# A new explicit order for the first task list of a fused attention and state-space kernel

## The chip, the cores and the metric

The kernel runs on one core of a Trainium2 chip. Time is device microseconds of one execution. The core's engines are TensorE (PE, with its weight loads PEld), VectorE (DVE), ScalarE (ACT), GpSimd (POOL) and SyncE (SP). Each engine takes its instructions strictly in the order in which the program lists them, and waits at an instruction until what that instruction depends on is there; everything behind it on that engine waits too. DMAs are issued from three queues here: SP's, POOL's and a few from ACT's.

## The reference

The input `x` has 2048 rows of 640. Two branches read it, and a gate mixes them:

```python
g = sigmoid((x * gate_w).sum(-1, keepdims=True))
a = attention(x)       # 32 heads of 20; each position sees 8 keys, 0, 2, .. 14 rows back
b = state_space(x)     # convolution with K[d, l] = Re sum_n C dt B exp(dt A l), plus x * Dskip
out = g * a + (1 - g) * b
```

Attention is `qkv = x @ wqkv`, a softmax over the eight logits of each position and head, the weighted sum of values, and `@ wo`. The state-space branch builds K for 640 channels and 2048 lags from 192 complex modes per channel, and convolves by an FFT of length 4096. All is in bfloat16 with float32 sums.

## The kernel before, in words

The work is cut into small tasks. A task has a name, an engine (or a choice of ACT and DVE), the tasks it depends on, the ring slots that it takes and releases, and a function that writes its instructions. There are two lists. The first has 1090 tasks, ends with the first FFT stage, and is what the change touches; the second has 237 (the rest of the convolution, the mix and the stores) and is the same before and after.

The order of the first list is written out by hand: `SEQ1` is a string of task numbers. `Plan.order` walks it, and a letter A or D behind a number says on which of ACT and DVE that task runs. `Plan.emit` calls the tasks in that order and ties each engine's instructions to the one before, so that no later stage reorders them:

```python
for k in self.pr["seq"]:
    t = self.tasks[int(k.rstrip("AD"))]
    t.eng = k[-1] if k[-1] in t.dur else next(iter(t.dur))
```

So the string decides three things: the order on each of PE, ACT, DVE, POOL and SP; which evictions run on ACT and which on DVE; and, with them, which waits are exposed.

The tasks that the text speaks of, with their numbers:

- 0 to 73 are the parameters of the state-space branch, on ACT and DVE. `mk` rounds a piece on ACT, `sp` (SP, line 614) writes it to `Sprm` in DRAM; sp9 is task 73, the last. `lin` (line 597 on DVE, 599 on ACT) are linear steps of this part, free to run on either.
- L00 and L01 (516, 517; SP, line 721) load the two halves of the first argument matrix L from `Sprm`; L10 and L11 (562, 563) the second, and so on to L91. `arg` (PE, line 748) multiplies by L, `act` (ACT, lines 760 and 762) takes sine or exponential, `pq` (DVE, lines 783 to 785) multiplies both, three instructions in one task, `kmm` (PE, line 801) contracts. There are ten chunks; pq92 (982) is the last product, fin9 (984) collects the last chunk.
- `late` (PE, line 291) are the 60 projections to q, k and v, `lev` their evictions. lst02, lst12, lst22 and lst32 (POOL, line 317; lst12 is 156) store v to `vS` in DRAM. gst (227) stores the gate row `omS`. halo1 to halo3 (POOL, line 312; halo2 is 177) copy keys over a block edge.
- wld (221; POOL, line 263) loads `wo` with two DMAs.
- `vc` (POOL, line 345) loads a block of shifted values from `vS` with two DMAs: vc0 (228), vc256 (264, the "second vc"), on to vc1280 (408), vc1536 (444) and vc1792 (480). Two buffers.
- The attention core has eight blocks of 256 rows. `prod` (DVE, line 351; five per block; prod74 is 489, the last) multiplies q and k, `lg` (PE, line 357) sums the heads, ast0 (244) stores the probabilities and asb0 (245) reads them back spread over partitions (SP, lines 396 and 401), `pv` (DVE, line 420; pv00, pv02, pv04 for block 0, pv50 is 426, pv60 is 462) weighs the values and needs both `asb` and `vc`, `oT` evicts (512 or 256 columns), `wo` projects (wo700 is 507), `ga` scales and evicts 320 columns on ACT (line 453) or DVE (line 455).
- The kernel K is expanded in two halves: shift, move, near, own, other (other0 is 750, other1 is 989), then `xst` stores X to `Kx` in DRAM and `xld` loads `kc` back (xst0 751 and 752, xld0 753 and 754, xst1 990 and 991, xld1 992 and 993; one of each pair on SP, one on POOL, lines 875, 873 and 881).
- rows0 to rows7 (995 to 1002; POOL, line 946) load `Usb`, the rows of x for the FFT. rows0 waits for prod74, since `Usb` takes the memory that q and k had; each later one first copies two elements of the block before (`pace`, line 945), so that it goes out only after that block has landed.
- `f1`, `fu` and `fk` (PE, line 1232) are the first FFT stage of the first half of K, of x and of the second half of K, ten, twenty and ten of them; `f1e`, `fue` and `fke` evict 1024 columns on ACT or DVE (lines 470 and 472).

When the last of these has released its PSUM, the second list starts with the `fp` matmuls (line 1009).

Of the kernel before, what the change touches and what calls it, by code (L numbers as in the profile page):

```python
# [62 lines left out]
0 2 3 1 6 8 4 14 13 26 5 7 27 9 10D 11D 12 18 74 76 28 75A 77A 78 79A 82 80 83D 15 17 23 81A 114 115D 120 94 56 121D 19 20 21 88 116 95A 89A 117A 37 100 92 104 101A 29  # L63
105A 93A 22 24 34D 35D 31 36 39 42 108 109A 25 86 118 106 90 119A 102 107A 32 103A 87A 110 96 84 16 38 30 111A 135 45 97A 40 33 46 41 136A 98 99A 43 44 229 51D 52 47 53
60 62D 122 146 85A 123A 57 147A 91A 125 129 230 126A 61 63 112 48 130A 113A 50 231 59 64A 152 154 153A 65A 155A 67 139 222 232 66 233 49 58 69 54 140A 68 70 55 71 72 234
127 137 73 235 128A 236 143 237 138A 223 144A 516 238 133 265 239 131 134D 240 148 267 224 132A 241 242 150 225 149A 151A 226 243 266 269 517 244 563 562 245 518 520 268
141 270 519 521 271 522 524 272 523 273 994 124 221 145 228 264 156 525 274 526 528 167 275 301 168D 142A 527 529 276 530 532 531 533 178 534 536 180 535 537 179A 303 538
540 539 541 175 181D 246 176D 186 542 544 277 278 543 545 187A 279 182 546 548 302 304 157 554 305 307 547 183A 549 158A 159 184 160A 306 308 550 552 551 553 185D 309 337
173 280 609 281 608 227 177 188 310 564 566 171 311 174A 565 312 567 313 172A 161 314 568 570 162A 569 571 556 315 339 165 572 574 338 573 575 166D 341 555 340 576 577
578 342 169 343 345 579 170A 163 580 582 199 581 583 584 586 585 587 557 344 346 558 588 590 589 591 200A 249 164D 559 347 600 373 203 592 594 593 204A 595 348 210 211A  # L70
205 560 596 598 206D 375 561 349 597 207 208D 350 201 351 189 602 599 202A 190A 610 612 611 613 601 374 376 377 614 616 247 615 617 379 618 620 191 248A 619 621 622 624
378 380 197 623 192A 625 626 628 252 381 605 409 198A 627 629 603 604 630 631 632 606 633 634 635 382 636 216 212 411 383 607 637 213D 646 316 655 352 654 317 638 217A
639 640 384 250 642 641 385 251A 643 644 645 214 386 656 648 387 195 215A 657 658 660 647 253 410 412 196A 659 661 254A 701 700 388 662 664 663 665 193 194A 282 651 413
666 667 668 255 257 670 256D 218 669 671 672 673 649 674 675 285 258D 415 219D 676 677 650 678 679 414 680 681 682 259 683 684 686 685 687 652 688 689 692 417 416 209 300
690 418 702 691 703 704 261 705 260A 706 708 283 707 709 710 653 694 445 419 262A 288 711 712 693 714 713 715 284D 447 697 716 718 717 719 695 720 721 722 420 724 723 725
755 756 263 353 726 727 286 289 728 729 730 696 732 731 733 734 698 421 735 318 287D 290D 738 699 736 291 737 757 758 759 760 739 761 762 422 763 765 764 766 740 423 743
# [1235 lines left out]
```

## Time and profile before

| | |
|---|---|
| median of three runs | 361.38 us (357.0 to 361.77) |
| the profiled execution | 360.97 us, of which the span is 359.0 us |
| DVE busy | 311.5 us, 87% of the span |
| ACT busy | 303.0 us, 84% |
| PE busy | 293.7 us, 82% |
| POOL busy | 78.3 us, 22% |
| first list, from the span's start to the first `fp` matmul | 283.3 us |

Times within the profile are counted from the span's start. A row of the timeline has the start, the duration, the engine, the line, the operation and its operands (out<-in), and in brackets how long the engine stood idle before and what ended that. SPq, POOLq and ACTq are the sequencers that issue DMAs: such a row is the issuing alone, and the transfer lands later. A row of the groups has the busy time and the mean of one instruction in nanoseconds, then the idle time before them.

### The profile page before, as it was taken

What the parts mean: (1) busy time and instruction counts of PE and PEld (TensorE: products, weight loads), DVE (VectorE), ACT (ScalarE), POOL (GpSimd) and SP (SyncE); (2) the same over time, 40 slices, a digit from 0 to 9 for tenths busy, and PEclk for the clock granted to TensorE, in tenths of its full rate; (3) what the DMA queues carried; (4) which work ended last, traced back from release to release, by engine and by line L of the source; (5) the groups of instructions that cost most, each with busy time, mean ns of one, the idle gap of its engine ahead of it and who ended that gap; (6) DMA issues with size and microseconds to landing.
All of it is one profiled execution on the core that took longest, in us unless ns stands there. A gap on an engine that the chain in (4) does not pass through costs nothing. (4 is left out here: it accounts for less than half of the span.)

```text
span 359.0 us, 12203 instructions
## 1 busy us (share of the span) xinstructions
PE 293.7 (82%) x5271; PEld 173.4 (48%) x5286; DVE 311.5 (87%) x413; ACT 303.0 (84%) x417; POOL 78.3 (22%) x125
## 2 busy tenths in 40 slices
PE   0199999699999999888887869999997799978760
PEld 0065564234544545445443424566664556647650
DVE  2899999669999899999998987999993479999982
ACT  1699997578989999999997979999895599888881
POOL 8930090211020100100012122416010023310032
PEclk9999999989999999999998978999998899999995
DMA  7951289421501611461256867489653149943047
GB/s 259 370 175 57 82 213 268 120 66 19 150 11 27 122 40 19 140 129 30 71 109 192 190 152 137 95 177 256 172 153 101 38 126 225 228 95 75 4 98 199
DMA packets 44042, 46.60 MB, mean 130 GB/s; under 512 B 24517, under 2 KB 38133, under 8 KB 43733
## 3 DMA queue, kind: packets, MB, share of 16 engines
q1 hardware_dynamic: 36116, 24.43, 26.2%
q0 software_dynamic: 5840, 20.55, 22.5%
q10 hardware_dynamic: 2032, 0.85, 0.9%
q8 instruction: 41, 0.67, 0.8%
q14 instruction: 13, 0.10, 0.1%
HBM read 31.31 MB, written 14.51 MB: 128 GB/s over the span
## 5 line engine op out<-in xcount | busy, mean ns | idle before, releaser
L291 PE MATMUL tb<-bufA 128*128 128x512 bf16 x285 | 71.7, 387 | 2.8 <-issue 1.1
L748 PE MATMUL ar<-Rarg,L 64*128 64x304 bf16 (+1 forms) x480 | 55.3, 282 | 14.7 <-ACT big L760 5.9
L760 ACT ACTIVATE big<-ar 128x608 bf16<-128x608 int16 x96 | 59.0, 681 | 8.2 <-PE ar L748 5.7
L762 ACT ACTIVATE big<-ar 128x864 bf16<-128x864 f32 x60 | 50.3, 917 | 3.6 <-PE ar L748 3.3
L291 PEld LDWEIGHTS <-bufA 128*128 128x128 bf16 x300 | 33.2, 120 | 31.7 <-issue 9.3
L420 DVE TENSOR_TENSOR pv<-vc,asb 128x4096 bf16<-128x4096 bf16 (+1 forms) x24 | 46.3, 1928 | 1.4 <-PE tb L426 1.4
L748 PEld LDWEIGHTS <-L 64*128 64x128 bf16 x480 | 21.4, 94 | 48.8 <-issue 41.9
L1009 PEld LDWEIGHTS <-PHI 128*128 128x128 bf16 x288 | 26.8, 99 | 18.0 <-issue 8.4
L801 PE MATMUL kps<-qq,pt 128*32 128x22 bf16 (+1 forms) x2560 | 26.3, 175 | 4.2 <-issue 4.2
L444 PE MATMUL tb<-wo_sb,oT 128*128 128x320 bf16 x160 | 28.1, 311 | 0.0
L801 PEld LDWEIGHTS <-pt 128*32 128x32 bf16 (+1 forms) x2560 | 22.5, 91 | 11.6 <-issue 8.7
L351 DVE TENSOR_TENSOR prod<-qk 128x2048 bf16<-128x2048 bf16 x20 | 24.1, 1220 | 2.9 <-PE lg L357 2.8
L351 DVE TENSOR_TENSOR prod<-prj 128x2048 bf16<-128x2048 bf16 x20 | 24.0, 1219 | 0.6 <-PE lg L357 0.5
L345 POOL DMA_DIRECT2D vc<-vS x16 | 11.5, 725 | 57.1 <-DVE pv L420 54.0
L426 PE MATMUL tb<-pv,ind 128*64 128x512 bf16 (+1 forms) x192 | 22.4, 361 | 0.2
L785 DVE TENSOR_TENSOR qq<-big 128x1408 bf16<-128x1408 bf16 x24 | 21.2, 885 | 0.0
L470 ACT ACTIVATE bufA<-bp 128x1024 bf16<-128x1024 f32 x16 | 16.0, 1032 | 5.6 <-PE bp L1232 5.5
L1009 PE MATMUL fp<-big,PHI 128*128 128x320 bf16 x112 | 17.9, 304 | 3.0 <-ACT sp_u L470 3.0
L200 PE MATMUL ar<-ident,xn 128*128 128x128 bf16 x80 | 8.1, 263 | 15.0 <-DMA xn<-in_A_x_dram 14.3
L470 ACT ACTIVATE sp_u<-fp 128x1280 bf16<-128x1280 f32 x14 | 17.3, 1237 | 3.4 <-PE fp L1009 3.4
L470 ACT ACTIVATE prj<-tb 128x512 bf16<-128x512 f32 x28 | 17.1, 612 | 3.1 <-PE tb L291 3.0
L470 ACT ACTIVATE big<-bp 128x1024 bf16<-128x1024 f32 x19 | 18.6, 1023 | 1.0 <-PE bp L1232 0.8
(173 smaller groups left out, 587.2 us busy)
## 6 DMA issues: line engine op xcount, KB each, us to landing
vc<-vS POOLq DMA_DIRECT2D x16, 327.5 KB, 6.9
PHI<-c_phi POOLq DMA_DIRECT2D x8, 384.0 KB, 4.9
Sprm<-pc SPq DMA_DIRECT2D x12, 240.0 KB, 2.0
L<-Sprm SPq DMA_DIRECT2D x80, 36.0 KB, 2.6
xn<-in_A_x_dram SPq DMA_DIRECT2D x4, 640.0 KB
gaS<-ga SPq DMA_DIRECT2D x8, 320.0 KB, 3.0
Usb<-in_A_x_dram POOLq DMA_DIRECT2D x8, 320.0 KB, 5.0
gaF<-gaS SPq DMA_DIRECT2D x8, 320.0 KB, 7.3
```

The source lines that it names most:

```text
L291: nc.tensor.matmul(ppf, self.wq[:, kt, which * D + e:(which + 1) * D:5], self.xT[:, c0 // 1024, kt, c0 % 1024:c0 % 1024 + SC], start=(kt = ...
L351: nc.vector.tensor_tensor(b[e][:], self.part(ch, 0)[:, e, o:o + C].unsqueeze(1).to_broadcast([128, W, C]), win(self.part(ch, 1)[:, e, :], ...
L420: nc.vector.tensor_tensor(b["pv", e][:, 0:2 * n], taps, aw, ALU.mult)
L426: nc.tensor.matmul(b["op", e][64 * a:64 * a + 64, 0:n, :], self.twin, b["pv", e][:, a:2 * n:2, w, :], start=(w == 0), stop=(w == HV - 1), ...
L444: nc.tensor.matmul(apf[:, :320], b["oT"][:, e, i * 128:(i + 1) * 128], wo_sb[:, e, hf * 320:(hf + 1) * 320], start=(e == 0), stop=(e == 4))
L470: nc.scalar.activation(o, i, ACT.Identity)
L748: nc.tensor.matmul(ar[:, g2, a0:a0 + ncol], L[rows, sb, gp, l0:l0 + 128], R[rows, c0:c0 + ncol], start=True, stop=True, tile_position=(64 ...
L760: nc.scalar.activation(dst[:, 2 * gp:2 * gp + 2, sub, :], ar[:].bitcast(I16)[:, :, 0:2 * SW:2], ACT.Sin, scale=SCL)
L762: nc.scalar.activation(dst[:, 2 * gp:2 * gp + 2].rearrange("p g s n -> p g (s n)"), ar[:, :, 0:2 * EW], ACT.Exp)
L785: nc.vector.tensor_tensor(qq[:], trg[:, :, KI:].rearrange("p a (v m) -> p a v m", v=2), exq[:, :, KI:].unsqueeze(2).to_broadcast([128, 32, ...
L801: nc.tensor.matmul(kps[32 * g:32 * g + 32, h, NM * ql:NM * ql + NM], pt[rows, k, v, :], qq[rows, k, v, :], start=(g not in started), stop= ...
L1009: nc.tensor.matmul(o.rearrange("p (c x) -> p c x", x=32), phis[fb][:, fl, kind, :], B[:, :, 2 * f1 + ri].rearrange("p c q g -> p c (q g)") ...
```

## The change

`SEQ1` is replaced by another order of the same 1090 tasks. No task is added, removed or altered. Of the tasks that can run on ACT or DVE, 55 change: 29 go from DVE to ACT and 26 from ACT to DVE, so that ACT runs 330 tasks of the list where it ran 327, and DVE 217 where it ran 220. On PE, ACT and DVE most tasks move by a few places; the largest regroupings are in the diff's stretches below. The order on the two queues that carry the transfers changes as follows (only the parts that differ most are listed):

```
POOL before: consts lst02 wld halo1 vc0 vc256 lst12 gst halo2 lst22 halo3 vc512 lst32 vc768 vc1024
             xst0 xld0 rows0 rows1 rows2 vc1280 rows3 rows4 rows5 vc1536 rows6 rows7 (gates, phi) vc1792 xst1 xld1
POOL after:  consts lst02 vc0 halo1 lst12 gst halo2 wld vc256 lst22 halo3 vc512 lst32 vc768 vc1024
             xst0 rows0 rows1 rows2 rows3 xld0 rows4 vc1280 rows5 rows6 vc1536 rows7 (gates) vc1792 (phi, a gate) xst1 xld1
SP before:   .. sp4 sp8 sp7 sp9 L00 L01 ast0 L11 L10 asb0 ast1 .. L50 L51 gaS0 asb3 L60 L61 ast5 L70 L71 gaS1 asb4
             xst0 L81 L80 ast6 xld0 L91 gaS2 L90 asb5 gaS3 asb6 ast7 ..
SP after:    .. sp4 sp7 sp8 sp9 L00 L01 ast0 L11 asb0 L10 ast1 .. L50 L51 ast3 gaS0 L61 L60 L71 L70 asb3 ast5 asb4 gaS1
             L80 L81 ast6 L91 gaS2 xst0 L90 asb5 xld0 ast7 gaS3 asb6 ..
```

At the end of the list, the order of the `fu`, `wo7` and `fk` matmuls and the sides on which `fke` are evicted change too; all ten `fk` and four `wo7` stay at the end, and wo700 now stands ahead of the first `fk`.

```diff
--- the order before
+++ the order after
@@ SEQ1 @@
...
-127 137 73 235 128A 236 143 237 138A 223 144A 516 238 133 265 239 131 134D 240 148 267 224 132A 241 242 150 225 149A 151A 226 243 266 269 517 244 563 562 245 518 520 268
-141 270 519 521 271 522 524 272 523 273 994 124 221 145 228 264 156 525 274 526 528 167 275 301 168D 142A 527 529 276 530 532 531 533 178 534 536 180 535 537 179A 303 538
-540 539 541 175 181D 246 176D 186 542 544 277 278 543 545 187A 279 182 546 548 302 304 157 554 305 307 547 183A 549 158A 159 184 160A 306 308 550 552 551 553 185D 309 337
-173 280 609 281 608 227 177 188 310 564 566 171 311 174A 565 312 567 313 172A 161 314 568 570 162A 569 571 556 315 339 165 572 574 338 573 575 166D 341 555 340 576 577
...
-827 828 322 456 829 797 830 831 832 457 325 747 748A 833 458 834 835 799 836 837 323D 483 839 326A 750 459 800 424 847 848 299 389 751 894 893 460 220 336 372 752 849 327
-838 850 851 482 852 841 485 853 484 854 855 840 857 856 858 859 486 861 860 487 328D 489 862 842 863 329 331 865 844 330D 864 866 867 869 488 868 871 870 873 843 872 874
-875 877 333 876 878 879 881 880 882 845 354 332D 885 846 887 883 884 895 897 490 896 899 898 901 886 900 903 902 905 355 334A 904 906 491 357 360 356D 890 907 908 909 910
-753 940 335 939 425 888 911 912 913 915 914 916 492 917 918 919 920 358 361 921 889 923 922 359D 362D 390 924 925 891 927 926 929 363 928 930 941 942 943 365 931 364D 892
-366D 933 945 944 946 932 947 367 949 948 493 368D 950 951 952 369 953 391 955 393 934 392D 396 936 954 956 370A 935 494 957 371 754 995 996 997 408 998 999 1000 444 1001
-1002 958 959 394 960 961 963 397 395A 962 964 398A 937 965 967 966 968 399 1010 400A 1011A 401 969 1026 402A 970 403 971 405 495 938 977 979 404D 426 406D 429 1027A 972
-973 974 1024 1025A 978 1022 1023A 980 1014 1015A 1012 427 1013A 1028 1029A 461 496 407 428D 432 975 430 976 1018 431D 1019A 982 462 1016 433 434A 981 1020 435 1017A 1021A
-1032 1033A 1030 437 1031A 1036 983 1037A 436D 1034 439 1064 438D 465 984 440D 985 1035A 1042 1065A 441 986 1043A 987A 1044 1066 1045A 1067A 463 1054 442D 988 989 464D 468
-1055A 497 443 990 1038 466 1004 1006 1009 1005 1008 1007 1003 480 991 993 1039A 1050 469 1062 467D 1051A 470D 1063A 498 1068 471 1040 473 1069A 1041A 472D 992 1046 1048
-475 474A 1047A 1049A 501 476A 477 1060 1056 1061A 478D 1057D 499 479 1058 1052 502 504 500A 1059A 1053A 505 503A 506D 1074 1070 507 1075A 1071D 1082 509 1080 508D 1083A
...
+29 229 88 117A 30 118 87A 24 100 57 31 119A 230 58 101A 108 34D 25 39 110 35D 84 36 109A 111A 102 45 42 106 103A 43 40 96 107A 41 44 32 46 98 97D 51A 33 47 122 99A 89A 52
+112 123A 90 53 62A 124 125 113A 60 91A 146 126A 61 147A 148 48 63 129 149A 49 64D 228 152 130A 50 85A 135 65D 153A 59 137 136A 145 66 67 127 231 68 69 222 54 71 138A 55
+233 232 72 70 143 128A 235 73 234 144A 139 237 236 140A 238 516 131 223 239 154 265 132A 517 240 155A 224 150 241 267 225 151A 242 141 226 156 243 518 227 520 142D 519
+266 244 268 133 269 271 521 522 270 523 524 563 273 525 526 527 528 272 134D 529 274 530 301 532 531 167 245 533 275 534 536 177 562 178 535 168D 221 537 303 538 179A 540
+180 264 539 541 276 181D 186 277 246 175 187A 278 542 176A 279 544 182 543 545 302 280 183D 304 546 548 305 173 547 549 307 306 550 174A 552 157 551 309 608 553 308 310
...
+354 799 894 854 855 856 857 460 858 859 326D 841 860 861 484 327 862 863 329 485 864 865 800 486 866 487 867 868 869 840 328D 870 871 489 330A 873 331 872 844 874 995 875
...
+335 997 912 913 751 914 915 360 492 916 917 939 886 918 356D 888 493 890 919 921 358 425 920 889 359D 922 923 390 361 924 925 753 998 494 362A 927 926 363 754 931 928 929
+365 364A 930 941 891 393 942 943 367 366A 944 945 999 369 946 368D 947 892 408 949 948 370D 932 933 950 951 952 953 391 954 495 955 394 1000 392D 496 956 396 957 934 958
+959 395D 961 960 397 936 962 371 963 461 398A 965 964 935 966 1026 426 1001 1014 1027A 399 444 1015A 401 977 967 400A 969 937 968 403 970 402A 1010 429 404A 1022 1011A
+405 427 1023A 938 406A 971 979 1024 407 972 1002 978 1025A 973 430 974 432 975 428A 1028 976 980 462 497 431A 981 1003 1006 1005 480 1029A 1012 433 1007 1013A 1018 1004
+434D 982 1019A 1016 435 1017A 1020 437 1008 465 1021A 1009 1030 436A 1036 1031A 983 439 1037A 984 438D 1032 985 986 440D 1033A 988 441 987A 1044 1066 1045A 463 442D 1067A
+989 443 1040 1041A 1048 468 990 991 466 464A 1049D 1050 469 1051A 467D 1064 498 470A 1034 1065A 471 1035A 473 1054 472D 1038 474D 1055A 475 1039D 992 993 1068 476D 1060
+1069A 501 477 1061A 1058 499 1059A 478D 1062 500A 504 479 1042 1063A 502 1043A 1056 503D 505 1057A 1052 506D 1046 1053A 507 1047A 1086 508D 509 1087D 1072 510A 511 1073A
+1076 512D 1080 1077A 513 1081A 1074 514D 1075D 515 1082 1083A 1084 1070 1085D 1071A 1078 1088 1079D 1089A
```

26 lines of the change are left out of this document (13 added, 13 removed).

## The prediction

> **What bounds the kernel now.** The page first. The span is the profile's; the execution took 360.97 us, 1.97 us more, and the median of the three runs is 361.38 us, so a sum made against 360.97 holds for both. No unit is full over the span, so the time must be read by stage.
>
> ```profile
> span 359.0 us, 12203 instructions
> PE 293.7 (82%) x5271; PEld 173.4 (48%) x5286; DVE 311.5 (87%) x413; ACT 303.0 (84%) x417; POOL 78.3 (22%) x125
> ```
>
> The table of stretches tells more. Behind each stretch stand its length and then the busy time of TensorE, weight loads, VectorE (DVE), ScalarE (ACT) and GpSimd (POOL), the granted clock, the DMA share and GB/s.
>
> ```profile
> 0.00:60.00 60.00, 41.08 (x310) 24.48 (x315) 51.43 (x59) 47.48 (x62) 28.59 (x44) 1.00 0.64 201
> 60.00:80.00 20.00, 16.38 (x97) 6.75 (x98) 13.42 (x20) 12.36 (x21) 3.24 (x7) 0.91 0.43 121
> 80.00:198.00 118.00, 106.13 (x2419) 56.07 (x2427) 114.40 (x159) 110.81 (x167) 11.06 (x16) 0.99 0.34 81
> 198.00:258.00 60.00, 53.32 (x1335) 31.27 (x1335) 55.79 (x80) 55.22 (x79) 17.31 (x28) 0.94 0.72 164
> 258.00:284.00 26.00, 21.57 (x259) 14.45 (x258) 17.70 (x19) 19.32 (x23) 1.78 (x3) 0.91 0.39 127
> ```
>
> The first list ends at 284. Up to there DVE has 252.7 us of work in 284 and ACT 245.2. From 80 to 258 DVE idles 7.8 us of 178 and ACT 12.0, so a reordering has little to win there. The holes are 60 to 80 (DVE idle 6.6, ACT 7.6) and 258 to 284 (8.3 and 6.7). The first 60 us wait for inputs that the list doesn't set; the last 75 belong to the second list, which is untouched. So holes worth 15 us bound the gain, and only part of them can close.
>
> **The hole at 60 to 80.** The SP queue writes the last parameter pieces, then loads L from them; the first `arg` matmuls need that L.
>
> ```profile
> 56.06 0.32 SPq L614 DMA_DIRECT2D Sprm<-pc  x1
> 63.78 4.23 SPq L721 DMA_DIRECT2D L<-Sprm  x8
> ...
> 75.28 1.20 SPq L401 DMA_DIRECT2D asb<-aS  x2
> ...
> 45.19 1.51 POOL L263 DMA_DIRECT2D wo_sb<-in_A_wo_dram  x2
> ...
> 50.28 2.86 POOL L345 DMA_DIRECT2D vc<-vS  x4
> ...
> q0 software_dynamic: 741, 2.77, 69.8%
> q1 hardware_dynamic: 807, 1.39, 25.9%
> ...
> Sprm<-pc SPq DMA_DIRECT2D x6, 240.0 KB, 7.7
> ```
>
> The last write is issued at 56.06 and L only at 63.78: 7.7 us between, and the writes of 46 to 62 have a median landing of 7.7. In that stretch (its three rows stand last) the Pool queue q0 moved 2.77 MB and q1 of SP 1.39. Of the 2.77, `wo_sb` (two of 400 KB at 45.19) and the second `vc` pair (two of 327.5 KB, the later half of the row at 50.28) are 1.455 MB that only the first output projection and the second `pv` block read, both long after 80. DVE pays in rows like these (what it waited for stands in brackets); the last is pv00, the first use of asb0:
>
> ```profile
> 78.09 0.69 DVE L472 CAST prj<-tb 128x512 bf16<-128x512 f32 x1 [2.17 <-ACT big L760]
> 78.69 2.28 DVE L420 TENSOR_TENSOR pv<-vc,asb 128x4096 bf16<-128x4096 bf16 x1
> ```
>
> **The change, part by part.** Work is the same: the same 1090 tasks, 18 table loads in both. 55 evictions and linear steps change engine, 29 from DVE to ACT and 26 back. Durations:
>
> ```profile
> L472 DVE CAST oT<-tb 128x512 bf16<-128x512 f32 x10 | 6.9, 686 | 2.9 <-PE tb L426 2.7
> ...
> L455 DVE TENSOR_SCALAR ga<-tb,g_sb 128x320 bf16<-128x320 f32 x20 | 10.8, 546 | 1.9 <-PE tb L444 1.9
> ...
> L472 DVE CAST prj<-tb 128x512 bf16<-128x512 f32 x7 | 4.8, 685 | 2.2 <-ACT big L760 2.2
> ...
> L472 DVE CAST oT<-tb 128x256 bf16<-128x256 f32 x4 | 1.7, 420 | 1.3 <-PE tb L426 1.3
> ...
> L420 DVE TENSOR_TENSOR pv<-vc,asb 128x4096 bf16<-128x4096 bf16 x16 | 36.5, 2282 | 0.3 <-PE tb L426 0.3
> ```
>
> *Step 1, parameters.* Pool now stores lst12 and omS and runs halo2 before it loads wo and the second vc, so 1.455 MB leave the way of the Sprm writes. The stretch moved 4.16 MB in 16 us, 0.26 MB per us: 5.6 us of transfer. Against it, DVE has two more things ahead of sp9: net one eviction of 0.685 and prod03 (1.23, the duration of prod74 in the row at 196.39 below), so 1.9 us later. Upper end: 5.6 - 1.9 = 3.7 earlier. Lower end: nothing, where other traffic keeps the writes slow. Behind it, the displaced 1.455 MB meet asb0, which pv00 needs. SP now issues asb0 before L10, and DVE has two more evictions (1.4 us) ahead of pv00, so 1.4 us of a late asb0 are covered. I take -2.5, nearer the upper end, because the row at 50.28 lies squarely on the writes.
>
> *Step 2, up to prod74.* The Usb chain starts when prod74 ends. Ahead of prod74 DVE has pv30 more (2.28), one 320-column `ga` more (0.546), one short `oT` more (0.42) and one 512-column `oT` less (0.686): +2.6. That work is moved, not added; if step 3 doesn't give it back, it is lost.
>
> *Step 3, prod74 to other1.* other1 finishes X and releases the last expansion. Ahead of it DVE has 23 moved pieces less and 18 more: `ga` 4 fewer (2.2), 512-column `oT` 2 fewer (1.4), short `oT` one more (0.4), the rest level: -3.1 over the whole list, so -5.7 behind prod74. ACT's sum ahead of it is level: the five pieces net that it takes over against three `fu` evictions that go behind. But POOL bounds this stretch: rows0 to rows7 each wait for the one before, and `vc` loads stand between.
>
> ```profile
> 196.39 1.23 DVE L351 TENSOR_TENSOR prod<-prj 128x2048 bf16<-128x2048 bf16 x1
> 197.53 0.69 DVE L783 TENSOR_TENSOR pt<-big 128x1024 bf16<-128x1024 bf16 x1
> 198.13 0.69 DVE L784 TENSOR_TENSOR pt<-big 128x1024 bf16<-128x1024 bf16 x1
> ...
> 198.31 0.82 POOL L946 DMA_DIRECT2D Usb<-in_A_x_dram  x1 [1.44 <-DVE prod L351]
> ...
> 206.20 0.81 POOL L946 DMA_DIRECT2D Usb<-in_A_x_dram  x1
> ...
> 231.59 1.43 POOL L345 DMA_DIRECT2D vc<-vS  x2 [1.25 <-DVE pv L420]
> ...
> 242.12 0.79 POOL L946 DMA_DIRECT2D Usb<-in_A_x_dram  x1
> ...
> L946 POOL DMA_DIRECT2D Usb<-in_A_x_dram x8: 787/790/819, 198.3 to 242.1; - x8
> L945 POOL COPY pace<-Usb x7: 177/185/1624, 206.0 to 241.9; 32x2 bf16<-32x2 bf16 x7
> ...
> DMA to landing us min/median/max: 4.3/5.0/7.6
> ...
> vc<-vS POOLq DMA_DIRECT2D x16, 327.5 KB, 6.9
> ...
> 248.52 2.28 DVE L420 TENSOR_TENSOR pv<-vc,asb 128x4096 bf16<-128x4096 bf16 x1
> ```
>
> prod74 ends at 197.62, rows0 is issued 0.7 later, rows7 at 242.12: seven spacings of 6.26 us on average. The pair of `vc` loads that pv60 reads (vc1536) goes out at 231.59, before rows6, and pv60 starts only at 248.52, the last row. In the new order it stands behind rows6, while pv60 moves ahead of pq92. Counted from prod74's end: rows6 at 0.7 + 6 x 6.26 = 38.3, vc1536 0.8 later, its second half 0.73 behind, landed 6.9 after: 46.7. From pv60's start to other1's end (257.72, the row at 256.99 below) DVE took 9.2 us; now pq92 stands in between too (three products, some 2.0 at the 0.60 of the rows at 197.53 and 198.13 and a longer third), a short `oT` more and one `ga` less: 11.1. So other1 ends 57.8 after prod74; before it was 257.72 - 197.62 = 60.1. Gain 2.3, though DVE's list alone would give 5.7: the rest goes to the wait behind Pool. Queued behind the waiting pv60 is all of DVE, and for pq92 behind it wait PE's last `kmm` and the expansion. xld0 of the first half also moves, in between rows3 and rows4; its issues fit into POOL's wait for rows3. Bounds: with the 5.0 landing in the Usb row a spacing of 5.8, gain 5.1; with the longest, 7.6, a spacing of 8.4, a loss of 10.5.
>
> *Step 4, the tail.*
>
> ```profile
> 256.99 0.73 DVE L847 COPY X<-nxt 128x80 bf16<-128x80 bf16 x3
> ...
> 272.78 1.24 PE L1232 MATMUL bp<-F1c,kc 64*128 64x128 bf16 x16 [2.37 <-DMA kc<-Kx]
> ...
> 283.30 2.03 PE L1009 MATMUL fp<-bufA,PHI 128*128 128x320 bf16 x7 [1.11 <-ACT bufA L470]
> ```
>
> From other1's end at 257.72 the store and load of Kx take until 272.78, 15.1 us, then ten `fk` with four `wo` take 10.5 until the second list's first matmul at 283.30. The change puts three more `fu` evictions and wo700 into those 15.1 us, where PE waits 2.37 (bracket of the row at 272.78). The last 10.5 us held 14 pieces, 0.75 each; one leaves: -0.7, bounds 0 and -1.5 (two pieces). What hides the three `fu` is the wait for kc; where they run over 15.1, the end moves by that.
>
> *The rest* of the new order, which shifts most instructions by a few places on their engine, changes which of PE, ACT and DVE is early at a hand-over. From 80 to 198 it could win DVE's 3.6 us of idle there, or lose about as much in two waits like the 2.17 at 78.09. I take 0.
>
> Sum: -2.5 + 2.6 - 2.3 - 0.7 = -2.9, against 360.97: **358.1 us**.
>
> The Trainium skill ("SBUF — State Buffer", two separate sides) says that a Pool-issued DMA can't write its descriptors while VectorE holds the shared port in a two-port mode, 620 ns becoming some 3100. By that figure the two more issues that now stand ahead of vc1536 would cost 5 us, an estimate. This trace differs: the eight Usb issues took 787 to 819 ns beside a DVE that was busy 55.79 of 60 us.
>
> **The rivals.**
> *The gain is handed back (no change).* For it: the 2.6 us ahead of prod74 stay if the Usb spacing is 6.8 instead of 6.26, as step 3 then loses 6 x 0.54 - 2.3 = 0.9; with step 1 at -1.5 and the tail at 0 the sum is +2.0. Against it: the first spacing, 198.31 to 206.20, had kc loads beside it that are now elsewhere. Time 360 to 363.
> *Everything closes (faster).* Step 1 at -3.7, step 3 at -5.1, the tail at -1.5 with +2.6: -7.7, 353.3. For it: ACT has 12 us of idle up to 258 to draw on. Against it: ACT's work ahead of other1 is not less, and all three must hit.
> *Pool's queue becomes the bound (slower).* vc1280 and vc1536 stand behind five and seven Usb-paced issues. It decides against the change from a spacing of 6.75 us on, where step 3 loses the 0.6 that steps 1 and 4 keep over step 2. At 8.4 it is -2.5 + 2.6 + 10.5 - 0.7 = +9.9: 370.9. For it: the first spacing was 7.9, and the displaced Kx traffic lands among the rows. Against it: the median landing of 5.0.
> *Pool's issues wait for DVE (slower).* One `pace` copy took 1624 ns against 185. If each of the two xld0G issues now ahead of vc1536 waited one pv of 2.28, other1 comes 4.6 later than forecast: 362.7. Against it: the Usb row. The skill's rule above is this one.
>
> **How the numbers follow.** Chances: forecast 0.44 (354 to 360), handed back 0.27, everything closes 0.15, Pool bound 0.11, port 0.03. 2% is 7.2 us, about what this kernel's runs can tell from no change (they spread from 357.0 to 361.77): faster is below 353.8, slower above 368.2. Faster: 0.12 of the third case and 0.05 of the forecast's tail, 0.17. Slower: most of the Pool bound, 0.09. Within: 0.74. The range goes from 351.0 (third case and 2 us) to 366.0, where half of the Pool case is left out.
>
> **What would show it.** Step 1: L is issued less than 5 us behind the last Sprm write, at 60 to 61.5, and 60 to 80 shows more than 15 us of DVE. Step 2: prod74 ends near 197.6 despite 2.6 more work. Step 3: idle time ahead of pv50 or pv60 and other1 at 55 to 60 us behind prod74. Step 4: less than 1 us of PE idle for kc. The prediction is wrong if L stays at 63 or later, if the Usb spacing leaves 5.5 to 6.9, or if ACT idles in the middle stretch by more than its present 7.2 us.

## The result, and the profile after

The changed kernel takes **372.81 us** (median of four runs, 370.08 to 374.1) against 360.29 us before (357.0 to 361.77): a ratio of 1.035, 95% interval 1.0253 to 1.0448. The forecast was 358.1 us in 351.0 to 366.0; the sign is wrong and the time lies outside the range. The profiled execution took 374.1 us with a span of 372.3 (before 360.97 and 359.0). The ratios below go against runs of the kernel before on the same chip at the same time, whose median lay between 359.99 and 363.38, and leave out disturbed runs, so they can differ a little from a quotient of medians.

The page of the changed kernel first:

```profile
span 372.3 us, 12228 instructions
PE 303.0 (81%) x5286; PEld 175.4 (47%) x5286; DVE 310.8 (83%) x410; ACT 305.2 (82%) x420; POOL 79.3 (21%) x125
...
L762 ACT ACTIVATE big<-ar 128x864 bf16<-128x864 f32 x60 | 50.2, 927 | 11.5 <-PE ar L748 11.5
L420 DVE TENSOR_TENSOR pv<-vc,asb 128x4096 bf16<-128x4096 bf16 (+1 forms) x24 | 46.3, 1928 | 11.8 <-DMA asb<-aS 5.6
...
L801 PE MATMUL kps<-qq,pt 128*32 128x22 bf16 (+1 forms) x2560 | 27.1, 176 | 10.2 <-issue 10.2
```

VectorE (DVE) and ScalarE (ACT) have the work that they had. TensorE (PE) shows 9.3 us more busy time for the same matmuls. Some of that is the record (the trace of before misses 15 of the 300 projections of line 291); the mean granted clock fell from 0.961 to 0.935. Two groups have idle time that they did not have or had less of: the `pv` products wait for asb0, and the `kps` matmuls wait for something put down to "issue", 10.2 us against 4.2 before. The stretches of the forecast (length, busy PE, PEld, DVE, ACT, POOL, granted clock, DMA share, GB/s), and one of them cut finer:

```profile
60.00:80.00 20.00, 17.27 (x121) 7.90 (x120) 13.33 (x21) 15.59 (x25) 7.54 (x11) 1.00 0.72 154
80.00:198.00 118.00, 104.83 (x2242) 51.95 (x2241) 110.30 (x150) 104.60 (x158) 9.58 (x14) 0.93 0.31 71
198.00:258.00 60.00, 48.55 (x1321) 27.02 (x1311) 49.26 (x59) 49.56 (x75) 17.21 (x28) 0.93 0.66 151
258.00:284.00 26.00, 25.43 (x347) 16.61 (x344) 21.61 (x34) 22.13 (x28) 2.88 (x5) 0.91 0.61 181
...
80.00:90.00 10.00, 7.34 (x46) 2.37 (x45) 7.40 (x7) 4.25 (x6) 0.00 (x0) 0.66 0.17 30
```

Before, 80 to 198 held 114.40 us of DVE and 198 to 258 held 55.79; now it is 110.30 and 49.26. The hole did not close, it moved. Three places show how, in the timeline of the changed kernel (start, length, engine; in brackets the idle time before and what ended it):

```profile
58.11 3.65 SPq L721 DMA_DIRECT2D L<-Sprm  x8
...
70.04 1.20 SPq L401 DMA_DIRECT2D asb<-aS  x2
...
67.00 2.29 POOL L263 DMA_DIRECT2D wo_sb<-in_A_wo_dram  x2
68.37 2.25 POOL L345 DMA_DIRECT2D vc<-vS  x2
...
79.85 2.29 DVE L420 TENSOR_TENSOR pv<-vc,asb 128x4096 bf16<-128x4096 bf16 x1 [5.56 <-DMA asb<-aS]
...
82.66 1.04 PE L357 MATMUL lg<-prod,ind 128*32 128x512 bf16 x8 [4.59 <-DVE rs L391]
83.64 0.90 PE L748 MATMUL ar<-Rarg,L 64*128 64x216 bf16 x8
```

L goes out at 58.11 instead of 63.78, and asb0 at 70.04 instead of 75.28. But wo_sb and the second `vc` pair go out at 67.00 to 70.6, just ahead of asb0. asb0 lands 9.8 us after its issue, DVE stands still for 5.56 us, and pv00 starts 1.2 us *later* than before. TensorE runs dry for 4.59 us and comes back at a granted clock of 0.66: the eight `ar` matmuls of 64x216, 0.54 us at full clock, take 0.90.

```profile
234.38 1.45 POOL L345 DMA_DIRECT2D vc<-vS  x2
...
241.84 2.29 DVE L420 TENSOR_TENSOR pv<-vc,asb 128x4096 bf16<-128x4096 bf16 x1 [3.26 <-issue]
254.61 2.29 DVE L420 TENSOR_TENSOR pv<-vc,asb 128x4096 bf16<-128x4096 bf16 x1 [2.69 <-DMA vc<-vS]
...
191.31 0.51 PE L801 MATMUL kps<-qq,pt 64*32 64x22 bf16 x44 [2.43 <-issue]
231.30 0.34 PE L801 MATMUL kps<-qq,pt 128*32 128x22 bf16 x26 [2.23 <-issue]
244.13 0.41 PE L801 MATMUL kps<-qq,pt 128*32 128x22 bf16 x35 [1.88 <-issue]
256.42 0.43 PE L801 MATMUL kps<-qq,pt 64*32 64x22 bf16 x35 [3.15 <-issue]
```

pv50 and pv60 wait for `vc` pairs that stand behind the Usb rows. vc1280 only goes out at 234.38; the profile names no cause for the idle time ahead of pv50, but the second of its two loads lands at 241.76, just before pv50 starts. TensorE stands still four times ahead of `kps` groups without a named cause. The clock shows the price of such a stop; here is the last of them in stretches of 2 us:

```profile
254.00:256.00 2.00, 0.00 (x0) 0.00 (x0) 1.39 (x1) 0.27 (x1) 2.00 (x4) 1.00 1.10 252
256.00:258.00 2.00, 1.58 (x49) 1.27 (x50) 0.90 (x1) 0.53 (x1) 0.76 (x2) 0.50 1.05 192
258.00:260.00 2.00, 2.00 (x23) 1.24 (x20) 1.54 (x3) 1.45 (x3) 0.69 (x2) 0.50 1.10 206
260.00:262.00 2.00, 2.00 (x15) 0.96 (x14) 2.00 (x3) 1.49 (x3) 0.42 (x1) 0.50 0.98 268
```

The milestones: pv00 +1.2 us against before, prod74's end 205.01 (+7.4), other1's end 268.94 (+11.2), and the last evictions of list one 11.9 later. Another 1.4 us come in the second list, which the change does not touch (75.7 us before, 77.1 now; 77.1 in h2 and 76.9 in the last mended kernel below as well). Their cause is not shown.

### The profile page after: what moved, and what is told of

Its sections match the earlier page's. It is cut to its first block, busy times and chain, and to the rows that moved or that the text cites. A ratio compares the mean times of both kernels' runs of the same rounds, so it can differ in the third digit from the quotient of the medians.

```text
span 372.3 us, 12228 instructions
## 1 busy us (share of the span) xinstructions
PE 303.0 (81%) x5286; PEld 175.4 (47%) x5286; DVE 310.8 (83%) x410; ACT 305.2 (82%) x420; POOL 79.3 (21%) x125
## 5 line engine op out<-in xcount | busy, mean ns | idle before, releaser
L291 PE MATMUL tb<-bufA 128*128 128x512 bf16 x300 | 74.5, 386 | 2.2 <-ACT bufA L470 0.6
L420 DVE TENSOR_TENSOR pv<-vc,asb 128x4096 bf16<-128x4096 bf16 (+1 forms) x24 | 46.3, 1928 | 11.8 <-DMA asb<-aS 5.6
L801 PE MATMUL kps<-qq,pt 128*32 128x22 bf16 (+1 forms) x2560 | 27.1, 176 | 10.2 <-issue 10.2
L444 PE MATMUL tb<-wo_sb,oT 128*128 128x320 bf16 x160 | 28.9, 316 | 0.1
L426 PE MATMUL tb<-pv,ind 128*64 128x512 bf16 (+1 forms) x192 | 25.4, 393 | 0.0
L345 POOL DMA_DIRECT2D vc<-vS x16 | 12.7, 854 | 53.5 <-DVE pv L420 49.6
L1009 PE MATMUL fp<-bufA,PHI 128*128 128x320 bf16 x112 | 19.0, 315 | 3.4 <-ACT sp_k L470 1.9
L470 ACT ACTIVATE sp_k<-fp 128x1280 bf16<-128x1280 f32 x14 | 17.3, 1237 | 5.0 <-PE fp L1009 4.8
L1042 DVE TENSOR_TENSOR ta<-sp_u,sp_k 128x1280 bf16<-128x1280 bf16 (+1 forms) x18 | 13.4, 750 | 8.1 <-ACT sp_u L470 6.2
L357 PE MATMUL lg<-prod,ind 128*32 128x512 bf16 x160 | 16.0, 416 | 4.7 <-DVE rs L391 4.6
L470 ACT ACTIVATE big<-bp 128x1024 bf16<-128x1024 f32 x18 | 17.5, 1026 | 2.8 <-PE bp L1232 2.7
```

Of the source, the lines that this page charges most:

```text
L291: nc.tensor.matmul(ppf, self.wq[:, kt, which * D + e:(which + 1) * D:5], self.xT[:, c0 // 1024, kt, c0 % 1024:c0 % 1024 + SC], start=(kt = ...
L420: nc.vector.tensor_tensor(b["pv", e][:, 0:2 * n], taps, aw, ALU.mult)
L426: nc.tensor.matmul(b["op", e][64 * a:64 * a + 64, 0:n, :], self.twin, b["pv", e][:, a:2 * n:2, w, :], start=(w == 0), stop=(w == HV - 1), ...
L444: nc.tensor.matmul(apf[:, :320], b["oT"][:, e, i * 128:(i + 1) * 128], wo_sb[:, e, hf * 320:(hf + 1) * 320], start=(e == 0), stop=(e == 4))
L470: nc.scalar.activation(o, i, ACT.Identity)
L801: nc.tensor.matmul(kps[32 * g:32 * g + 32, h, NM * ql:NM * ql + NM], pt[rows, k, v, :], qq[rows, k, v, :], start=(g not in started), stop= ...
```

## The experiments

**The two orders apart.** Two mixtures: the compute order of one kernel (TensorE, VectorE, ScalarE and the engine of each eviction) with the transfer queues (SP and Pool) of the other. In the sketch P, A and D are the orders on TensorE, ScalarE and VectorE, S and G those on SP and Pool.

```
h1:  P A D of before   S G of after
h2:  P A D of after    S G of before (SP up to L10 as after)
```

> The order of TensorE, VectorE and ScalarE, and the engine of each eviction, from the kernel before; the order of the two transfer queues (SP and Pool) from the changed kernel. Theory T (the transfer queues make the loss: asb0's collision and vc1280 and vc1536 behind the Usb rows): 367 to 372, with a hole ahead of pv50 or pv60. Rival O (the new order of the computing engines makes it): 358 to 362. Rival F (each order fits its own transfers only, so that both mixtures lose): over 370.

> The other mixture: the order of TensorE, VectorE and ScalarE and the engines of the changed kernel; the two transfer queues in the order of the kernel before (SP's stores and loads up to L10 stay as changed, since the pieces they read are made in that order). Theory T: L late again, no wait longer than 1 us ahead of pv50 and pv60, 361 to 365 (the 2.6 us of VectorE work that moved ahead of prod74 and some of the 5 us of the first hole remain). Rival O: 370 to 374. Rival F: over 370 too.

h1 took 367.82 us, ratio 1.0246 (1.0170 to 1.0323); h2 took 360.91, ratio 1.0032 (0.9977 to 1.0087). Theory T holds: the transfer queues make the loss, the new compute order costs nothing that can be measured (h2 came out just below the 361 to 365 expected of it). In h1 the hole lies ahead of pv00 (6.58 us of DVE idle), not ahead of pv50 or pv60 as expected: with the order of before, pv60 comes late enough. The two, 2.5% and 0.3%, add up to the changed kernel's 3.5% within their intervals.

**Step 1 alone, and step 1 without its collision.** Pool's order, the kernel before and the experiment:

```
-  lst02 wld halo1 vc0 vc256 lst12 omS halo2 lst22 ...
+  lst02 vc0 halo1 lst12 omS halo2 wld vc256 lst22 ...
```

> The kernel before, with one part of the change: Pool issues lst12, omS and halo2 ahead of wo_sb and the second vc pair; everything else stays. Theory C (the two loads now collide with the weights asb0 that the first pv product reads): L is issued near 58 instead of 63.8, but asb0 lands only near 80, pv00 starts within 1 us of the 78.7 it had, PE gets a low granted clock behind the hole, and the time is 359 to 363. Rival G (the step is a gain as forecast, and the loss is made later): pv00 starts near 75 and the time is 356 to 358.

368.14 us, ratio 1.0260 (1.0127 to 1.0394). This one step makes the larger part of the loss, and more than theory C gave it, whose pv00 within 1 us of before did not come either. L goes out at 59.55, asb0 at 72.76, but:

```profile
81.85 2.29 DVE L420 TENSOR_TENSOR pv<-vc,asb 128x4096 bf16<-128x4096 bf16 x1 [6.90 <-DMA asb<-aS]
...
84.80 2.29 PE L291 MATMUL tb<-bufA 128*128 128x512 bf16 x5 [6.70 <-DVE qk L472]
```

and the stretch behind it, in the table of stretches:

```profile
80.00:90.00 10.00, 5.20 (x24) 1.60 (x24) 7.53 (x9) 2.16 (x3) 0.00 (x0) 0.50 0.16 28
```

asb0 takes 9.1 us to land, pv00 is 3.2 us later than before, and the clock is 0.50 from 80 to 90: five projections that take 1.24 us at full clock take 2.29. By pq02 it is 5.4 us behind.

The next kernel has the same order, with two tiny Pool copies that read an asb tile ahead of the two loads:

```
 def load_wo(self):
+    gpsimd.tensor_copy(hold, asb[0:32, 0:2]); gpsimd.tensor_copy(hold, asb[64:96, 0:2])
     ...
```

> As the kernel before, with Pool's order of the change, and two tiny Pool copies that read asb0 in front of wo_sb and the second vc pair, so that both are issued only when asb0 has landed. Theory C: L near 58, asb0 lands 3 to 4 us behind its issue, pv00 starts at 74 to 76, and with nothing lost behind it the time is 355 to 358. Rival G gives the same pv00 as in the kernel without the copies, and no more than 1 us between the two. A third view, that an early start up there is eaten by the next wait (the middle stretch is bound by work that was already early), gives pv00 at 75 and a time of 359 to 362.

356.48 us, ratio 0.9925 (0.9883 to 0.9968): faster than the kernel before by 0.75%, as theory C said, with pv00 half a us later than its 74 to 76. The copies in fact read the asb tile of the second block, so wo_sb went out at 93.61 only, and still in time. asb0, issued at 73.13, lands 3.4 us later, and the clock stays whole (timeline, then the stretch 80 to 90):

```profile
76.53 2.29 DVE L424 TENSOR_TENSOR pv<-vc,asb 128x4096 bf16<-128x4096 bf16 x1 [1.03 <-DMA asb<-aS]
```
```profile
80.00:90.00 10.00, 10.00 (x77) 4.63 (x76) 9.68 (x14) 7.42 (x12) 0.00 (x0) 1.00 0.15 30
```

3.4 us against 9.1 and 9.8: that is what the two loads do to asb0. L is 5.8 us earlier than before and pv00 2.2: between them stand this 1.03 and what the other engines still need.

A further turn, with asb0 also issued ahead of L10:

> The kernel that took 356.48 (before with wo_sb and the second vc pair held back until an asb tile has landed), and SP issues asb0 right behind L11, ahead of L10. asb0 goes out 2 us earlier, so the 1.03 us that pv00 still waited for it go: 355 to 356.5, 0.986 to 0.991 of the kernel before. If L10 is late by it, no gain: 356.5 to 358.

359.58 us, ratio 0.9950 (0.9881 to 1.0020). pv00 starts at 73.87, 2.7 us earlier still, but between prod74 and other1 its trace loses 3.2 us again; DVE waits there 0.8 to 1.2 us for TensorE in five places, where the kernel of 356.48 has two such waits. The time is told apart neither from the kernel before nor from that of 356.48 (0.9925), so no gain is shown; the 0.986 to 0.991 expected lies inside the interval.

**The price of the low clock.** 25 extra matmuls that keep TensorE busy over the hole of step 1 alone. The first try:

```
 def mm(...):                     # a late projection
+    if (sc, which, e) == (1, 2, 2):
+        for _ in range(25): matmul(spare, ident, wq[:, 0, 0:512])
```

> The kernel before with only the change's order of wo_sb and the second vc pair (the one that took 368.14), and in it 25 matmuls of 128x512 more, into a spare bank, in front of the projection at which TensorE stood still for 6.7 us while asb0 was on its way. They do no work for the result. Theory K (the low clock behind the hole has a price of its own): granted clock 1.00 from 80 to 90 instead of 0.50, pv00 as late as there (81.9), but pq02 3 to 3.5 us behind the kernel before instead of 5.4, and 1.5 to 2.6 us off the end: 365.5 to 366.6. Rival (VectorE and ScalarE set the pace there, the clock costs nothing): pq02 still 5.4 behind, 368 within 1 us.

367.97 us, ratio 1.0144 (1.0064 to 1.0225), and no answer: that projection stands at 64 us, before the hole, and the matmuls pushed everything by 5.6 us there. It still tells something: Pool's loads then went out at 76.15, behind asb0's 72.40, and pv00 waited for nothing. With the projection that stood still, (2, 2, 2):

> As the kernel with the 25 extra matmuls, but these now stand in front of the projection at which TensorE really stood still from 78.1 to 84.8 while asb0 was on its way (in the run before they stood in front of one at 64 and delayed it by 5.6 us). Theory K (the low clock behind a hole has a price of its own): granted clock 1.00 from 80 to 90, pv00 3.2 us behind the kernel before as without the matmuls, but pq02 3 to 3.7 behind instead of 5.4, and 1.5 to 2.5 us off the end of list one. Rival: pq02 still 5.4 behind.

Timeline of TensorE, then the stretch 80 to 90:

```profile
77.06 5.56 PE L291 MATMUL kps<-bufA,ident 128*128 128x512 bf16 x24
83.98 1.24 PE L295 MATMUL tb<-bufA 128*128 128x512 bf16 x5 [1.37 <-DVE qk L476]
...
129.32 1.91 PE L295 MATMUL tb<-bufA 128*128 128x512 bf16 x4 [3.28 <-issue]
```
```profile
80.00:90.00 10.00, 8.58 (x56) 3.79 (x54) 8.68 (x10) 3.25 (x5) 0.00 (x0) 1.00 0.10 15
```

Theory K holds up to pq02: clock 1.00, pv00 2.35 us behind and pq02 2.11 behind, where step 1 alone went from 3.16 to 5.39. So the low clock behind that hole costs 2.2 to 2.5 us, by one trace of each. Behind that a stop of 3.28 us put down to issue comes up, which step 1 alone did not have (its cause follows below), and the time is 367.96, ratio 1.0239 (1.0087 to 1.0390): at the end no gain is shown.

**The changed kernel mended.** First the held loads, then the late transfers (X store and load early, vc1280 between rows2 and rows3, vc1536 between rows5 and rows6), then both, twice.

> The changed kernel with the two tiny Pool copies that read asb0 in front of wo_sb and the second vc pair; all else as changed. Theory C (asb0's collision makes the first loss, and its hole lowers TensorE's clock for some us behind it): pv00 at 74 to 76 instead of 79.86, granted clock 1.00 from 80 to 90 instead of 0.66, and 6 to 8 us off the end: 364.5 to 367. Rival: the hole at 70 to 82 only moves to the next late piece, and less than 3 us come off: 370 or more.

366.97 us, ratio 1.0160 (1.0083 to 1.0238): pv00 at 74.81, clock 1.00 from 80 to 90, as theory C said, at the upper edge of its time. pv00 is 5.0 us earlier than in the changed kernel and prod74 5.5.

> The changed kernel with Pool's and SP's late transfers put back to the places of the kernel before: the X store and load of the first half early, vc1280 between rows2 and rows3, vc1536 between rows5 and rows6. The first hole stays. Theory R (vc1280 and vc1536 behind the Usb rows make the second loss): no wait over 1 us ahead of pv50 and pv60, prod74 to other1 58 to 60 us instead of 63.9, time 367 to 369.5. Rival P (the second loss is TensorE's and its clock's, the vc loads were only the last of several late things): 371 to 373.

369.80 us, ratio 1.0240 (1.0146 to 1.0334). Neither view is right. By the middle values 1.1% is gained, though the interval overlaps the changed kernel's own, and not by the way that theory R gave. pv50 starts 6.1 us earlier and no `vc` is waited for, but other1 only 1.2: prod74 to other1 takes 63.2 us against 63.9. TensorE is what is late now (timeline, then its row in the list of waits: total, times, longest):

```profile
248.95 1.23 DVE L420 TENSOR_TENSOR pv<-vc,asb 128x2048 bf16<-128x2048 bf16 x1 [3.09 <-PE tb L426]
251.24 2.29 DVE L420 TENSOR_TENSOR pv<-vc,asb 128x4096 bf16<-128x4096 bf16 x1 [1.07 <-PE tb L426]
255.99 0.42 DVE L472 CAST oT<-tb 128x256 bf16<-128x256 f32 x1 [2.46 <-PE tb L426]
```
```profile
PE kps L801 <- issue: 6.8, 5, 1.8
```

> Both of these edits in the changed kernel. If the two losses are separate and add up: the sum of the two gains, 359 to 363, that is no slower than the kernel before by more than 1%. By the 360.91 of the mixture with the transfer queues of before and the 3.5 us that holding the two loads won there: 357 to 359. If there is a third cause in the order of the computing engines: 364 or more.

Its four runs lay between 357.1 and 366.39 and settle nothing.

> The changed kernel with both edits once more (held loads, and Pool's and SP's late transfers in the places of the kernel before), as its four runs lay between 357.1 and 366.39. If transfers alone make the loss, 1.00 of the kernel before within 0.7%. If TensorE's late instructions hit it again ahead of other1, 1.01 to 1.02, with 5 us or more of idle time put down to issue.

359.27 us, ratio 1.0023 (0.9962 to 1.0084), prod74 to other1 57.4 us. Holding two loads and putting the late transfers back takes the whole loss away. Together they give 3.3% and one by one 1.9 and 1.1, which adds up within the intervals; on top of the held loads the late transfers give 1.4.

**What stands behind "issue".** The kernel before has this row among its waits (total, times, longest), and the changed one had 10.2 us of it.

```profile
PE kps L801 <- issue: 4.2, 3, 2.1
```

In every trace TensorE's idle stretches of over 0.8 us ahead of `kps`, put down to issue, have one thing in common. Count the matmul and weight-load rows in order of time (each is one instruction) up to the end of the stop: divided by 256 the count leaves 179 to 186 in every trace without missing rows. Some of them:

```
kernel    end of stop   instructions before     queue q8, packet before it
after     191.31        5049 = 19 x 256 + 185   188.23 to 189.79
after     231.30        6841 = 26 x 256 + 185   228.35 to 230.02
after     244.13        7351 = 28 x 256 + 183   241.48 to 242.48
after     256.42        7863 = 30 x 256 + 183   254.06 to 255.10
h2        205.61        5817 = 22 x 256 + 185   202.53 to 203.85
h2        244.57        7864 = 30 x 256 + 184   242.17 to 243.05
```

Queue q8, of kind instruction, moves 41 packets of 16 KB in the run, and 41 x 256 is about TensorE's 10,572 matmuls and weight loads. The number before the x is that of the packets that had come. So the packet of the next 256 instructions is there 1.3 to 1.8 us before the end of each stop: TensorE has run out of instructions. The label alone does not show this: step 1 alone has 3.03 us put down to issue ahead of a `bp` matmul that reads `Usb`, at 88 of 256. A packet starts about 1 us after TensorE has passed the border before it while the DMA engines are quiet (205.06 to 205.86), and 2.7 to 3.9 us after it ahead of the four stops (250.14 to 254.06). In that last wait, 250.14 to 256.43, the engines were full (their busy share in 40 slices, and the queues):

```profile
DMA  9995997999779796996989999999999693899999
...
q0 software_dynamic: 305, 0.88, 69.4%
q1 hardware_dynamic: 406, 0.56, 33.9%
q8 instruction: 1, 0.02, 1.0%
```

Without the stop the 256 instructions there, with many `kps` among them, last 3.1 to 4.6 us; the packet comes 4.2 to 5.0 us after the border. The Trainium skill ("Trainium Architecture — The Big Picture", The software stack) gives an instruction 64 bytes; 256 of them are the 16 KB of these packets. In this trace they come during the run.

Whether full engines alone do it was tried with traffic for nobody, where the kernel before has quiet engines:

```
 def halo(...):
+    if sc == 3: 3 x gpsimd.dma_start(junk[k], x[k])   # 655 KB each
```

> The kernel before, with three loads of 655 KB from x into an unused DRAM piece, issued by Pool behind halo3 at about 103. Nothing reads the piece. From 100 to 112 the kernel before has a DMA share of at most 0.17 and TensorE no idle time of note, and TensorE's queue q8 takes a 16 KB packet of instructions at 104 and at 110. Theory I (TensorE stands still with nothing that it waits for because its instructions come late through full DMA engines; this is the idle time put down to issue ahead of kps, 4.2 us in all before and 10.2 after): with the engines full from 103 to 113 one idle stretch of 1.5 us or more put down to issue appears there, next to a q8 packet, with a granted clock of 0.5 to 0.9 behind it, and the time is 362 to 366. Rival N (that idle time only happens to lie where transfers are dense): no idle stretch over 0.5 us put down to issue between 103 and 116, and 359 to 361, or a wait for a late L piece, named as such.

364.2 us, ratio 1.0135 (0.9941 to 1.0329), unclear as a time. The trace is for rival N at this place: no stop.

```profile
108.00:112.00 4.00, 3.95 (x43) 1.93 (x33) 3.93 (x9) 3.55 (x7) 0.26 (x1) 1.00 0.98 336
112.00:116.00 4.00, 3.95 (x89) 2.32 (x89) 4.00 (x6) 3.94 (x5) 0.00 (x0) 1.00 0.54 188
```

TensorE needs few instructions there, 43 matmuls in 4 us, and the packet came 2.7 us after the border, with 5.5 us until it was needed. Full engines are not enough; the border must also lie where instructions are short. That can be tried without moving any work: tiny matmuls in TensorE's idle time at the start shift every border.

```
 def window(...):
+    for _ in range(N): matmul(spare[0:32, 0, 0:1], ident[:, 0:32], ident[:, 0:1])
     # p1: before, N = 96    p0: before, N = 128    p2: after, N = 64
```

> The kernel before, its two orders untouched, with 96 tiny matmuls (32 columns of the identity by one column, into a spare bank, read by nobody) on TensorE ahead of its first transpose, where it stands idle from 2.75 to 15.07 us. With their weight loads they are 192 instructions. Theory I (TensorE gets its instructions in packets of 256 and stands still where it has run through one before the next has come): every packet border moves 192 instructions towards the start. In the trace of before the borders lie at instruction 185 of each 256 and hit two dense places; moved by 192 they fall into dense places near 121, 154, 219 and 238 us with full DMA engines. So several stretches of idle time put down to issue appear that were not there, each at instruction 185 of 256 in the new count, their sum is 8 us or more instead of 4.2, and the time is 364 to 374. Rival N (that idle time belongs to the matmuls' own data): idle stretches stay ahead of the same matmuls as before, and 359 to 362.

> The same with 128 tiny matmuls, 256 instructions: a whole packet. Theory I: the borders fall between the same two matmuls as before, the idle time put down to issue stays near 4 us ahead of the same two kps groups, and the time is that of the kernel before within 0.7%. If the tiny matmuls themselves did something (a later first transpose, another clock), it would show here as in the kernel with 96.

> The changed kernel with 64 tiny matmuls in the same place, 128 instructions. Theory I: no idle stretch stays at the four kps groups of the changed kernel's trace (its instructions 5049, 6841, 7351 and 7863, all at 183 to 185 of 256); new ones lie at 185 of 256 in the new count. Worked out from how fast each 256 instructions ran and how full the DMA engines were, about as much idle time arises at the new places, so 369 to 377. Rival N: they stay, 371 to 374.

p1: 370.85 us, ratio **1.0232** (1.0113 to 1.0351), for 2.72 us of matmuls in idle time. p0, with more of them but the borders in their old places: 363.47, ratio 1.0093 (1.0043 to 1.0142). The stops of p1 (timeline, then the row of its waits):

```profile
129.33 0.64 PE L804 MATMUL kps<-qq,pt 128*32 128x22 bf16 x59 [3.29 <-issue]
204.83 0.29 PE L804 MATMUL kps<-qq,pt 64*32 64x22 bf16 x18 [1.03 <-issue]
226.94 0.20 PE L804 MATMUL kps<-qq,pt 128*32 128x22 bf16 x1 [1.75 <-issue]
238.31 0.18 PE L804 MATMUL kps<-qq,pt 64*32 64x22 bf16 x1 [1.18 <-issue]
260.49 0.26 PE L804 MATMUL kps<-qq,pt 128*32 128x22 bf16 x14 [1.42 <-issue]
```
```profile
PE kps L804 <- issue: 8.7, 5, 3.3
```

The two of before (190.22 and 209.82) are gone, five others are there, 8.7 us in all; in the new count 173 of 256 stand before the end of the first and 165 to 170 before the others, with 16 matmul rows missing from that trace. Of the four places expected, three came within 6 us (126, 225 and 237 for 121, 219 and 238), that near 154 didn't, and two came that were not expected (204 and 259). In p0 one of the two old stops stays (194.34, 2.16 us); the other is not there, and one of 1.46 us stands at another border (228.28). Its 0.9% is more than the 0.7% expected, so not all of p1's 2.3% is the borders'; by the middle values 1.4% is, with some 1.3 either way. p2 took 375.31, ratio 1.0267 (1.0096 to 1.0438): the stops of the changed kernel are gone from their places, new ones end at 225.82 and 262.45, and the time is much the same. Theory I holds: these stops are TensorE's instruction supply. It also explains the stop of 3.28 us in the kernel with 25 extra matmuls. Those are 50 instructions and moved every border behind them; in the first try, whose trace misses no row, the same stop (3.37 us, ending at 129.99) has 2490 = 9 x 256 + 186 instructions before its end. So filling a hole with matmuls moves the borders too, and the end of those two kernels tells nothing about the clock.

## Why the prediction was wrong, step by step

At pv00, prod74's end, other1's end and the end of the first list the forecast's terms add up to -2.5, +0.1, -2.2 and -2.9 us; the profile has +1.2, +7.4, +11.2 and +11.9.

**Step 1** failed in its sign. Its mechanism was right and undersized: L came 5.7 us earlier, not 2.5, and the 1.9 us by which the last write was to be later did not show (55.60 against 56.06). What failed is the sentence "so 1.4 us of a late asb0 are covered" and the lower bound, "nothing": the displaced 1.455 MB were let off with a remark, while the very rows that showed them slowing the Sprm writes (a landing of 7.7 us) said what they would do to asb0. Landing 9.1 to 9.8 us after its issue instead of 3.4, asb0 is some 6 us late with 1.4 covered; the earlier L gives back most of it at pv00, and the low clock costs 2.2 to 2.5 more. Alone the step measured 2.6% slower, some 9 us; without its collision 0.75% faster, some 2.7 us. The sign that it offered, L less than 5 us behind the last write, came out (58.11 against 55.60) and says nothing of asb0; the other, over 15 us of DVE from 60 to 80, failed with 13.33.

**Step 2** was right in size. In h2, where the transfers are those of before, pv00 starts 0.1 us earlier and prod74 ends 1.8 later: the 2.6 us of moved work, less what small holes took in. In the changed kernel prod74 ended at 205.01 and not near 197.6 because of step 1: with the loads held it ends at 199.55, which is 5.5 of the 7.4 us, and the 1.9 that are left are what h2 shows.

**Step 3** failed: 63.9 us from prod74 to other1 against 57.8 forecast and 60.1 before. DVE's list alone was put at 5.7 us of gain. It gives 3.5 in h2 (56.6 us) and 2.7 with the mended transfers (57.4), where Pool has the order of before, so that term had the right sign and was too large. The Usb spacing was 6.6 us (46.3 over seven), within the 5.5 to 6.9 that the prediction allowed. Over the six spacings that count for vc1536 it was 6.8, just past the 6.75 from which the prediction itself saw a loss; its worst case, 8.4, did not come. What was missed: pv50 waits for vc1280, moved behind rows4, which the step never worked out (3.26 us), and Pool's last wait for vc1536 came 3 us later than its sum said (issued 42.2 us behind prod74's end instead of 39.1). But undoing this gives other1 only 1.2 us: TensorE's stops and its clock are as late. The rival "Pool's queue becomes the bound" gave 370.9 us, the nearest, but partly by luck: putting the late transfers back is worth 1.1% alone and 1.4% on top of the held loads, of 3.5%.

**Step 4** came to nothing: from other1's end on the changed kernel loses some 0.7 us where 0.7 was forecast as a gain. TensorE's wait for kc fell from 2.37 to 0.8 us, as the step said, but DVE then waits 3.14 us for `bp` at 286.06.

**"The rest, 0"** failed. It allowed about 3.6 us either way from 80 to 198 and thought only of hand-overs between three engines. Its sign of being wrong came: ACT idled 13.4 us in that stretch, against 7.2 before. Two prices were not in it. A hole on TensorE is followed by work at half the clock, 5.4 us of it behind the hole of step 1 alone: a lowered clock was in the profile before (0.91, 0.94 and 0.91 in three of its stretches) and was quoted without being priced. The Trainium skill ("TensorE: Matmul & The Clock Gate", Part 1) has the clock at half after an idle window of about 3.4 us and back after as long a busy one; here it fell 1.8 us into the hole of step 1 alone (78.1 to 79.9), sooner than that, and came back 5.4 us after its end (84.8 to 90.2). And the idle time of `kps` put down to issue, 4.2 us before, was in no term of the sum; it grew to 10.2.

**The port rival** fell: the two pieces of xld0 (a pair of `kc` loads, 1.15 us) and the Usb issues (0.79 to 0.82) took on Pool what they took before, beside a busy DVE.

What stays open: how the changed kernel's loss divides between asb0, the `vc` waits and the stops, as each of them sets off the others; the traces of the kernel that took 356.48 and of the mended one show only that without the first two the stops shrink as well (2.4 and 1.7 us of them ahead of `kps`). And the 0.9% of the kernel with 256 instructions more, whose borders are in their old places, has no cause that was shown.

## What to carry to other kernels

A load that is moved out of the way of one transfer is moved into the way of another: list what is in flight in its new place, and price the collision at the landing that the trace shows under load, not at the quiet one. Where a queue has time to spare, make the bulk load wait until the urgent small one has landed; that turned 2.6% slower into 0.75% faster. And read idle time with no named cause as a cause: dense runs of tiny matmuls beside full DMA engines starve TensorE of instructions, and each stop is paid again in its clock.

## What the runs showed of the hardware that was not expected

- TensorE gets its instructions during the run, 256 at a time in 16 KB packets through the same DMA engines as the data, one packet ahead. Under full engines a packet came 4.2 to 6.3 us after the border before it, against some 2 us when quiet. 192 tiny instructions at the start of the kernel, in idle time, made it 2.3% slower; 256 of them, 0.9%.
- A stop of TensorE costs more than itself: one hole of 6.7 us was followed by 2.2 to 2.5 us lost at a clock of 0.50, a third more, and with idle matmuls in the hole that part was gone by pq02. Between 30 us and the end of the first list, the low clock of step 1 alone, of before and of the changed kernel lasts 3.4, 6.8 or 10.2 us each time, so it is paid in such steps.
- asb0, two small loads of 128 KB on SP's queue, lands in 3.4 us alone and in 9.1 to 9.8 us behind 1.455 MB of Pool's queue, though the queues are different.
